# Windowed attention and a spatial-gating MLP on one core: another order of the same instructions, with score and PV groups of head pairs side by side

## The chip, the core and the metric

The kernel runs on one core of a Trainium2 chip. A core has five engines that work at the same time, each with its own queue that it takes strictly in order: TensorE (PE, matrix products; its weight loads are listed apart as PEld), VectorE (DVE), ScalarE (ACT), GpSimd (POOL) and SyncE (SP), which here only issues DMA transfers. Engines wait for each other by semaphores. Operands lie in SBUF; TensorE writes its results to PSUM, from where VectorE and ScalarE read them. The metric is the time of one execution in microseconds (us), as the median of several runs.

## The reference: what is computed

```python
scores = scale * np.matmul(q, k.transpose(0, 1, 3, 2))      # q, k, v: (8, 8, 576, 64), scale = 1/8
mask = (rel >= 0) & (rel < window)                          # rel = query - key, window = 64
scores = np.where(mask, scores, -1000000000.0)
...
attn = attn / (np.sum(attn, axis=-1, keepdims=True) + 1e-09)
return np.matmul(attn, v).astype(np.float32)                # x: (8, 576, 512) after heads are joined

h = np.maximum(x @ w_in, 0.0)                               # w_in: (512, 1024); u, v: its halves
v_n = (v - mu) / np.sqrt(var + 1e-06)                       # over the 512 columns of a row
v_s = np.einsum('ts,bsd->btd', w_spatial, v_n) + b_spatial[None, :, None]
gated = u * v_s
return (gated @ w_out).astype(np.float32)
```

For each of 8 batches: attention with a causal window of 64 positions in 8 heads, and on its result a layer with two weight products, a normalisation and a product over the 576 positions. Inputs and output are float32; the kernel computes its products from float16.

## The kernel before

The program is a list of small pieces of work. A string, ORDER, names 1195 of them as words; a loop at the end of the kernel (L653) takes the words in turn and calls the helper of each, which issues a few instructions. Dependencies are found by the framework from the tiles that are read and written. So ORDER settles one thing only: in which order each engine meets its instructions, each queue its transfers, and each buffer of a ring its tiles. A word ends in a letter where the engine of a copy can be chosen: A for ScalarE, D for VectorE, P for GpSimd.

The words, by stage, with b the batch:

- Loads on SP's queue: `l.b.q.s` and `l.b.k.s` (L297), `lv.b.n` (L313), the halves of w_in `wl.half.r` (L248); on GpSimd's queue `wsp` (w_spatial) and `wout`. `st.b.j` (L636) stores a result tile on SP's queue.
- Casts to float16: `c` (L326; batches 4 to 7 in two pieces of 128x1152, the earlier ones in five of 128x512), `cv` (L339), `wc` (L253). `sh` (L348) makes a copy of V that is shifted by 64 rows.
- Turning q and k so that the head dimension lies on partitions: in batches 0 to 3 by TensorE (`T`, L372, and the copy out of PSUM, `to`), in 4 to 7 by VectorE (`R`, L365).
- Attention, for a pair of heads s = 0 to 3, and s = 4 for the last 64 positions of all heads: `S` (L394) computes scores, with TensorE in 64*64 tiles in batches 0 to 3 and in 32*64 tiles in 4 to 7; `E` (L449, exp, ScalarE), `M` (L463, mask by a minimum, VectorE), `P` (L476) computes the sums of the softmax and the product with V, in tiles of 128*64; `n1`, `n2` (L499, L505, ScalarE) give the inverse of the sum as exp(-ln), `x` (L512, VectorE) multiplies it in.
- The layer: `V` (L526, products of x with the second half of w_in; `Q`, L534, does it for the last 64 positions beside the last `O` of the batch before, in two halves of the array, 128*64), `vo` (relu out of PSUM), `bs` (statistics, VectorE), `rs` (ScalarE), `ln` (normalise, VectorE), `U` (L584, first half of w_in) and `ru` (relu, ScalarE), `G` (L604, product over positions) and `g` (L615, VectorE), `O` (L622, w_out), `oc` (copy out of PSUM).
- `W` and `wo` turn w_spatial once. `H.n` (L641) issues n matmuls on zeros near the start.

`V`, `U`, `G`, `O`, `W` and `T` use TensorE's full 128*128 tile (the last 64 positions of `T` and the last slice of `G` have fewer rows).

Two rings of PSUM set limits to the order. Scores and PV results of s = 0 to 3 (and scores of s = 4) share two buffers with the tag "att", so each `S` or `P` waits until the tile two allocations before it has been read; nearly all else shares four buffers with the tag "mm" (L180).

## Time and profile before

| | |
|---|---|
| median of 11 runs | 212.97 us (211.97 to 213.71) |
| profiled execution, its own time | 214.61 us |
| its span, first to last instruction | 212.9 us |
| busy in it: PE, DVE, ACT, POOL | 199.1, 174.2, 163.7, 65.6 us |
| mean granted TensorE clock | 0.992 |
| start of the first `G` (G.0.1) | 40.96 us |
| DMA traffic | 41.47 MB, mean 195 GB/s |

How to read the lines that follow: `L486` is a line of the kernel; `oz<-e,onesK 128*64 128x512 f16 x2` is two instructions that write tile oz from tiles e and onesK, with 128 rows and 64 columns of the array active (128*64) and an operand of 128 partitions by 512 elements. In a timeline, the first number is the start and the second the time from the first start to the last end in us. TensorE's matmuls overlap: a 128x512 one lasts 0.38 us and the next one starts 0.216 us after it, so that the distance of starts, not the duration, is what one costs. Words and rows are matched by counting: TensorE's 2726 matmuls stand in the trace in ORDER's sequence.

### The profile page before, as it was taken

What the parts mean: (1) busy time and instruction counts of PE and PEld (TensorE: products, weight loads), DVE (VectorE), ACT (ScalarE), POOL (GpSimd) and SP (SyncE); (2) the same over time, 40 slices, a digit from 0 to 9 for tenths busy, and PEclk for the clock granted to TensorE, in tenths of its full rate; (3) what the DMA queues carried; (4) which work ended last, traced back from release to release, by engine and by line L of the source; (5) the groups of instructions that cost most, each with busy time, mean ns of one, the idle gap of its engine ahead of it and who ended that gap; (6) DMA issues with size and microseconds to landing.
All of it is one profiled execution on the core that took longest, in us unless ns stands there. A gap on an engine that the chain in (4) does not pass through costs nothing.

```text
span 212.9 us, 6682 instructions
## 1 busy us (share of the span) xinstructions
PE 199.1 (93%) x2726; PEld 106.9 (50%) x2726; DVE 174.2 (82%) x359; ACT 163.7 (77%) x305; POOL 65.6 (31%) x93
## 2 busy tenths in 40 slices
...
DMA packets 77742, 41.47 MB, mean 195 GB/s; under 512 B 44368, under 2 KB 72080, under 8 KB 77712
## 3 DMA queue, kind: packets, MB, share of 16 engines
...
q0 software_dynamic: 1168, 1.19, 3.7%
...
## 4 chain that ended last, share of the span: by engine, by line
PE 75%; SPq 7%; DVE 6%; ACT 5%; DMA 3%; issue 1%; POOL 1%; DVEq 0%
PE ps L612 19%; PE po L626 13%; PE pv L531 11%; PE pu L589 11%; PE oz L486 4%; SPq L317 4%; PE sc L421 4%; PE oz L496 4%; DMA wf<-in_moe_w_in_dram 3%; PE pv L543 3%; SPq L301 2%; PE sc L410 2%; PE pu L594 2%; DVE st L562 1%; ACT vs L556 1%
## 5 line engine op out<-in xcount | busy, mean ns | idle before, releaser
L612 PE MATMUL ps<-wspT,vn 128*128 128x512 f16 (+1 forms) x256 | 39.0, 286 | 0.6 <-DVE wspT L276 0.6
L453 ACT ACTIVATE e<-sc 128x1024 f16<-128x1024 f32 x32 | 32.6, 1024 | 3.5 <-PE sc L410 3.3
L531 PE MATMUL pv<-win,x 128*128 128x512 f16 x128 | 32.7, 392 | 0.4 <-DVE x L517 0.4
L517 DVE TENSOR_TENSOR x<-oz,zi 128x512 f16<-128x512 f32 (+1 forms) x40 | 25.0, 629 | 8.5 <-ACT zi L509 8.3
L626 PE MATMUL po<-wout,g 128*128 128x512 f16 x128 | 30.8, 379 | 0.0
L589 PE MATMUL pu<-x,win 128*128 128x512 f16 x128 | 30.5, 380 | 0.1
L502 ACT ACTIVATE ln<-oz 128x512 f32<-128x512 f32 (+1 forms) x40 | 21.8, 555 | 9.9 <-PE oz L496 9.9
L562 DVE BATCH_NORM_STATS2 st<-vs 128x6 f32<-128x512 f16 (+1 forms) x40 | 26.9, 674 | 0.5 <-ACT vs L556 0.2
L619 DVE TENSOR_TENSOR g<-ps,ru 128x512 f16<-128x512 f32 (+1 forms) x40 | 24.2, 628 | 3.5 <-PE ps L612 2.2
L469 DVE TENSOR_TENSOR e<-e,mask 128x1024 f16<-128x1024 f16 x32 | 23.3, 728 | 2.9 <-ACT e L453 2.6
L612 PEld LDWEIGHTS <-vn 128*128 128x128 f16 x256 | 17.0, 97 | 14.9 <-DVE vn L580 1.9
L556 ACT ACTIVATE vs<-pv 128x512 f16<-128x512 f32 (+1 forms) x32 | 18.6, 597 | 6.9 <-PE pv L531 6.2
L509 ACT ACTIVATE zi<-ln 128x512 f32<-128x512 f32 (+1 forms) x40 | 23.3, 590 | 0.6
L602 ACT ACTIVATE ru<-pu 128x512 f32<-128x512 f32 (+1 forms) x40 | 21.1, 558 | 2.5 <-PE pu L594 2.0
L360 POOL COPY vs<-vn 64x512 f16<-64x512 f16 (+1 forms) x15 | 13.0, 870 | 22.0 <-DVE vn L346 10.0
L531 PEld LDWEIGHTS <-x 128*128 128x128 f16 x128 | 11.7, 100 | 14.5 <-DVE x L517 1.8
L633 ACT COPY ob<-po 128x512 f32<-128x512 f32 (+1 forms) x21 | 12.1, 587 | 8.7 <-PE po L626 6.5
L589 PEld LDWEIGHTS <-win 128*128 128x128 f16 x128 | 11.7, 98 | 13.1 <-ACT vs L556 0.4
L626 PEld LDWEIGHTS <-g 128*128 128x128 f16 x128 | 11.5, 98 | 12.3 <-DVE g L619 0.7
L612 PE MATMUL ps<-wspT,vlast 65*128 65x512 f16 (+1 forms) x64 | 17.1, 288 | 0.0
L496 PEld LDWEIGHTS <-vn 128*64 128x64 f16 x320 | 13.6, 112 | 3.5
L486 PE MATMUL oz<-e,onesK 128*64 128x512 f16 x64 | 12.8, 396 | 2.4 <-ACT vs L351 1.3
...
## 6 DMA issues: line engine op xcount, KB each, us to landing
...
```

Of the source, the lines that this page charges most:

```text
L453: nc.scalar.activation(e2[:, :, :], sc[0][:, :, :], AF.Exp, bias=0.0, scale=0.125)
L469: nc.vector.tensor_tensor(e2[:, :, :], e2[:, :, :], m, ALU.min)
L496: nc.tensor.matmul(oz[64 * h:64 * h + 64, 0, c0:c0 + 64], vt, e2[:, h, c0:c0 + 64], start=True, stop=True)
L502: nc.scalar.activation(lnz[:, 0:n], OZ[b, s][:, 1, 0:n], AF.Ln)
L509: nc.scalar.activation(zinv[:, 0:n], lnz[:, 0:n], AF.Exp, bias=0.0, scale=-1.0)
L517: nc.vector.tensor_tensor(x[:, 0:n], oz[:, 0, 0:n], zinv[:, 0:n], ALU.mult)
L531: nc.tensor.matmul(PV[b, j][0:jn, :], xcol(b, r, j), w_in_sb[:, r, 512:1024], start=(r == 0), stop=(r == 3))
L562: nc.vector.bn_stats(st6[0:jn, 0:6], VSB[b, j][0:jn, :])
L589: nc.tensor.matmul(pu[:, :], w_in_sb[:, r, 128 * m:128 * m + 128], X[b, r][:, :], start=(r == 0), stop=(r == 3))
L612: nc.tensor.matmul(o, VN[b, kk][0:kn, 128 * mm_:128 * mm_ + 128], w, start=(kk == 0), stop=(kk == 4))
L619: nc.vector.tensor_tensor(g[:, :], ps[:, 0:n], RU.pop((b, m))[:, 0:n], ALU.mult)
L626: nc.tensor.matmul(po[:, :], G[b, r][:, 128 * j:128 * j + 128], w_out_sb[:, r, :], start=(r == 0), stop=(r == 3))
```

## The change

ORDER is replaced by another sequence of the same 1195 pieces of work; no helper changes. From batch 1 on, most score groups `S` of neighbouring head pairs follow each other directly in TensorE's order, and so do the PV groups `P` (`S.5.0 S.5.1`, `P.5.1 P.5.0`). Everything else moves with it: the other work of TensorE, the loads and stores in SP's queue, and the order on each engine. For 151 of the 285 copies and casts the engine is another one; by word, VectorE does 14 `to` in place of 25, 16 `vo` in place of 8, 5 `wc` in place of 1; ScalarE 26 `to` in place of 15 and 24 `vo` in place of 32.

The diff, cut to the start, two places in batches 5 to 7, and the end:

```diff
ORDER = """
-id scratch table l.0.q.1 keep H.2 l.0.q.0 mask l.0.k.3 H.3 l.0.k.0 small l.0.k.1 lv.0.0 H.3 lv.0.1
-c.0.q.1.A l.0.q.2 H.4 lv.0.3 c.0.q.0.P lv.0.4 H.2 l.0.k.2 T.0.q.0 T.0.q.1 to.0.q.0.A H.2 wl.1.1
-c.0.k.1.D c.0.k.0.A lv.0.2 to.0.q.1.A T.0.k.0 l.0.q.3 T.0.k.1 maskr to.0.k.0.D H.3 wl.1.0 to.0.k.1.D
-S.0.0 l.0.q.4 c.0.q.2.P cv.0.0.D E.0.0 S.0.1 lv.0.5 c.0.k.3.D E.0.1 sh.0.0.0.D T.0.k.3 l.0.k.4
-T.0.q.2 H.6 to.0.q.2.D sh.0.0.1.A c.0.k.2.P M.0.0 lv.1.0 P.0.0 cv.0.1.D M.0.1 n1.0.0 lv.0.7 T.0.k.2
-sh.0.1.0.A to.0.k.3.D lv.0.6 to.0.k.2.A sh.0.1.1.D P.0.1 c.0.q.3.D n2.0.0 lv.0.8 H.4 n1.0.1 x.0.0
-wl.1.3 n2.0.1 T.0.q.3 wl.1.2 cv.0.2.D S.0.2 c.0.q.4.A l.1.k.1 x.0.1 c.0.k.4.P to.0.q.3.A wl.0.3
-T.0.q.4 sh.0.2.1.D wc.1.1.P E.0.2 l.1.q.0 T.0.k.4 S.0.3 to.0.k.4.D to.0.q.4.D wl.0.2 wc.1.0.A M.0.2
-S.0.4 cv.0.3.P E.0.3 wl.0.0 V.0.3.0.1 V.0.3.1.2 l.1.k.0 sh.0.3.1.D sh.0.2.0.A P.0.2 cv.0.4.D E.0.4
-M.0.3 n1.0.2 V.0.0.0.1 M.0.4 V.0.0.1.2 wc.1.2.P V.0.2.0.1 sh.0.4.0.A V.0.2.1.2 sh.0.3.0.P P.0.3
-n2.0.2 n1.0.3 wc.1.3.P x.0.2 P.0.4 n2.0.3 wsp c.1.k.1.D wl.0.1 V.0.2.2.3 V.0.0.2.3 n1.0.4 lv.1.1
-x.0.3 V.0.3.2.3 n2.0.4 l.1.q.1 c.1.q.0.A wc.0.3.D V.0.3.3.4 lv.1.3 x.0.4 V.0.2.3.4 vo.0.3.A
-V.0.0.3.4 vo.0.2.D l.1.q.2 wc.0.0.A V.0.1.0.1 l.1.k.2 bs.0.3 V.0.1.1.2 vo.0.0.A V.0.1.2.3 l.1.k.3
-V.0.1.3.4 wc.0.2.A wc.0.1.P T.1.q.0 lv.1.2 vo.0.1.A Q.0 to.1.q.0.D c.1.k.0.P U.0.0 l.1.q.3 vo.0.4.A
-cv.1.0.D U.0.4 bs.0.2 ru.0.0 T.1.k.0 U.0.3 sh.1.0.1.D to.1.k.0.A bs.0.4 c.1.q.1.P ones.0 S.1.0
-ru.0.4 sh.1.0.0.D U.0.2 E.1.0 bs.0.0 l.1.k.4 U.0.1 bs.0.1 ru.0.3 ru.0.2 T.1.q.1 M.1.0 T.1.k.1 ru.0.1
-W.1 to.1.q.1.D rs.0 lv.1.5 W.0 wo.1.A ln.0.4 P.1.0 ln.0.2 to.1.k.1.A c.1.q.2.P W.4 wo.0.D n1.1.0
-lv.1.4 ln.0.1 S.1.1 W.2 ln.0.3 n2.1.0 ln.0.0 l.1.q.4 T.1.q.2 wo.4.A W.3 wo.2.D c.1.k.3.P E.1.1
-wo.3.D G.0.1 lv.1.6 wout x.1.0 lv.1.7 ones.1 to.1.q.2.D c.1.k.2.P G.0.4 l.2.k.0 M.1.1 T.1.k.2 G.0.2
...
-ru.4.3 l.6.q.4 G.4.0 x.5.1 E.5.2 l.6.k.2 cv.6.1.D S.5.4 M.5.2 S.5.3 st.3.4 E.5.4 g.4.0 G.4.2 E.5.3
-l.6.k.7 l.6.k.4 G.4.3 cv.6.2.A M.5.3 l.6.k.6 M.5.4 P.5.3 cv.6.3.D l.6.q.5 g.4.2 P.5.4 n1.5.3
-sh.6.1.1.P P.5.2 n1.5.4 g.4.3 O.4.1 n2.5.3 lv.6.0 sh.6.1.0.P n2.5.4 x.5.3 l.7.k.0 O.4.2 n1.5.2
-c.6.q.0.D oc.4.1.A c.6.k.0.P O.4.3 n2.5.2 x.5.4 st.4.1 oc.4.2.D l.7.k.2 U.5.4 x.5.2 l.7.k.1 G.4.4
-ru.5.4 c.6.k.1.P l.7.k.3 oc.4.3.A R.6.q.0 O.4.0 st.3.3 g.4.4 V.5.1.0.4 l.7.q.0 R.6.k.0 sh.6.4.0.P
-oc.4.0.D V.5.2.0.4 st.4.2 vo.5.1.A c.6.q.1.A bs.5.1 l.7.q.7 S.6.0 S.6.1 lv.7.2 R.6.k.1 E.6.0
...
-sh.7.1.1.P l.7.q.5 g.5.3 O.5.0 l.7.q.4 g.5.4 sh.7.4.0.P R.7.q.0 S.6.4 O.5.1 cv.7.1.P E.6.4 x.6.3
-sh.7.1.0.A oc.5.0.D S.7.1 M.6.4 S.7.0 oc.5.1.A c.7.k.1.D P.6.4 cv.7.0.P V.6.2.0.4 n1.6.4 E.7.0
-sh.7.0.1.P O.5.2 n2.6.4 vo.6.2.A x.6.4 V.6.1.0.4 oc.5.2.A M.7.0 U.6.4 R.7.k.1 st.5.2 vo.6.1.A
-V.6.3.0.4 st.4.0 E.7.1 bs.6.1 st.5.1 V.6.0.0.4 st.5.0 c.7.q.1.A sh.7.0.0.D P.7.0 Q.6 R.7.q.1 n1.7.0
-vo.6.0.A M.7.1 ru.6.4 S.7.2 vo.6.3.A oc.5.4.D U.6.2 E.7.2 bs.6.0 U.6.0 vo.6.4.A bs.6.2 ru.6.2 U.6.3
-bs.6.3 n2.7.0 ru.6.0 O.5.3 bs.6.4 ru.6.3 U.6.1 x.7.0 rs.6 ln.6.0 P.7.1 ln.6.2 ln.6.1 n1.7.1 S.7.3
-ln.6.3 oc.5.3.A ln.6.4 G.6.2 M.7.2 E.7.3 st.5.3 G.6.1 n2.7.1 g.6.2 ru.6.1 M.7.3 G.6.0 g.6.1 x.7.1
-G.6.3 g.6.0 S.7.4 g.6.3 O.6.0 E.7.4 M.7.4 P.7.2 oc.6.0.D P.7.3 P.7.4 G.6.4 n1.7.4 n1.7.2 O.6.1
-n2.7.4 n2.7.2 x.7.4 O.6.2 n1.7.3 oc.6.1.D g.6.4 n2.7.3 U.7.4 st.6.1 x.7.2 Q.7 st.5.4 ru.7.4 x.7.3
-oc.6.2.D V.7.0.0.4 vo.7.4.D st.6.2 V.7.1.0.4 bs.7.4 oc.6.4.A V.7.3.0.4 vo.7.0.A vo.7.1.D bs.7.0
-V.7.2.0.4 bs.7.1 O.6.3 vo.7.2.A vo.7.3.A bs.7.2 U.7.0 oc.6.3.A bs.7.3 U.7.2 st.6.3 st.6.0 rs.7 U.7.3
-st.6.4 ru.7.0 ln.7.3 U.7.1 ln.7.1 ru.7.3 ln.7.0 ln.7.2 ru.7.2 ln.7.4 G.7.2 ru.7.1 G.7.0 g.7.2 G.7.1
-g.7.0 G.7.3 g.7.1 G.7.4 g.7.3 O.7.0 g.7.4 O.7.1 oc.7.0.A st.7.0 O.7.2 oc.7.1.A st.7.1 O.7.3 oc.7.2.D
-st.7.2 Q.8 oc.7.3.D st.7.3 oc.7.4.A st.7.4
+keep l.0.k.0 mask l.0.q.0 maskr l.0.q.1 l.0.k.1 scratch table H.3 l.0.k.3 lv.0.1 l.0.q.2 H.4 lv.0.0
+c.0.k.0.P l.0.k.2 c.0.q.0.P l.0.q.3 H.2 id c.0.q.1.P lv.0.2 T.0.q.0 T.0.k.0 lv.0.3 to.0.q.0.A H.2
+c.0.k.1.A l.0.q.4 ones.1 T.0.k.1 to.0.k.0.A to.0.k.1.D c.0.k.3.A S.0.0 lv.0.4 small c.0.q.2.A
+T.0.q.1 H.3 to.0.q.1.D E.0.0 l.0.k.4 H.3 cv.0.0.D wl.1.1 c.0.k.2.D sh.0.0.1.P H.2 sh.0.0.0.D T.0.k.2
+c.0.q.3.A lv.0.5 S.0.1 M.0.0 wl.1.0 T.0.k.3 E.0.1 wl.1.2 P.0.0 cv.0.1.P lv.0.8 n1.0.0 M.0.1
+sh.0.1.1.P lv.0.7 c.0.q.4.A sh.0.1.0.D P.0.1 n2.0.0 lv.0.6 to.0.k.3.D to.0.k.2.A T.0.q.3 ones.0
+wl.0.2 T.0.q.2 c.0.k.4.D H.6 x.0.0 n1.0.1 wl.1.3 to.0.q.2.A to.0.q.3.D n2.0.1 wc.1.1.D T.0.q.4 S.0.2
+wc.1.0.P wl.0.0 x.0.1 T.0.k.4 E.0.2 H.4 wl.0.1 wc.1.2.D cv.0.2.D l.1.q.0 to.0.k.4.A S.0.3 to.0.q.4.D
+cv.0.4.D wl.0.3 V.0.2.0.1 E.0.3 V.0.2.1.2 M.0.2 S.0.4 l.1.k.0 V.0.0.0.1 sh.0.2.0.D V.0.0.1.2
+sh.0.4.0.A sh.0.2.1.D l.1.q.1 P.0.2 M.0.3 E.0.4 l.1.q.2 cv.0.3.D n1.0.2 sh.0.3.1.D n2.0.2 l.1.k.1
+sh.0.3.0.D P.0.3 M.0.4 n1.0.3 lv.1.1 wc.0.0.P x.0.2 P.0.4 n2.0.3 wsp wc.1.3.D lv.1.0 V.0.0.2.3
+V.0.3.0.1 x.0.3 V.0.3.1.2 V.0.3.2.3 c.1.q.0.A V.0.2.2.3 wc.0.1.D lv.1.2 V.0.0.3.4 wc.0.2.D n1.0.4
+V.0.2.3.4 V.0.3.3.4 vo.0.0.D vo.0.2.A n2.0.4 vo.0.3.D V.0.1.0.1 wc.0.3.A V.0.1.1.2 V.0.1.2.3 x.0.4
+c.1.k.0.A T.1.q.0 bs.0.3 V.0.1.3.4 to.1.q.0.A Q.0 U.0.0 c.1.q.1.D vo.0.1.A l.1.k.4 vo.0.4.A bs.0.1
+U.0.3 ru.0.0 bs.0.0 U.0.4 ru.0.3 T.1.k.0 bs.0.2 ru.0.4 T.1.q.1 c.1.k.1.P U.0.1 c.1.q.2.A to.1.k.0.A
+bs.0.4 T.1.k.1 ru.0.1 lv.1.3 U.0.2 to.1.q.1.D rs.0 lv.1.5 to.1.k.1.A ln.0.1 S.1.0 l.1.k.2 ln.0.4
+ru.0.2 S.1.1 ln.0.0 l.1.q.3 E.1.0 W.1 ln.0.3 ln.0.2 lv.1.4 W.0 wo.1.A T.1.q.2 cv.1.0.D l.1.q.4 W.3
+M.1.0 sh.1.0.0.A sh.1.0.1.P W.2 l.1.k.3 wo.0.D wo.3.A P.1.0 to.1.q.2.D c.1.k.4.P lv.1.7 wo.2.A W.4
+wout E.1.1 wo.4.D G.0.1 cv.1.1.P n1.1.0 lv.1.6 G.0.4 g.0.1 sh.1.1.0.P l.2.q.0 n2.1.0 G.0.2 lv.1.8
...
+E.5.2 g.4.0 G.4.2 lv.6.0 E.5.3 M.5.2 S.5.4 G.4.3 E.5.4 M.5.3 l.6.k.7 c.6.k.0.A M.5.4 P.5.3 g.4.2
+lv.7.3 P.5.2 cv.6.4.D P.5.4 n1.5.2 g.4.3 sh.6.4.0.P lv.7.2 O.4.2 n1.5.4 c.6.q.0.D cv.6.2.P n2.5.2
+G.4.4 n2.5.4 x.5.2 st.3.3 n1.5.3 O.4.3 cv.6.0.P st.3.4 x.5.4 n2.5.3 R.6.q.0 l.6.k.4 O.4.0 oc.4.2.A
+l.6.q.5 g.4.4 x.5.3 U.5.4 l.6.q.6 oc.4.0.A V.5.0.0.4 l.6.k.5 oc.4.3.D sh.6.1.0.A l.6.q.4 cv.6.1.D
+V.5.1.0.4 l.7.q.5 vo.5.0.D sh.6.0.0.P ru.5.4 R.6.k.0 V.5.2.0.4 st.4.2 vo.5.1.A sh.6.1.1.P l.6.k.6
+bs.5.0 S.6.0 vo.5.2.A lv.7.0 S.6.1 bs.5.1 cv.7.2.A cv.7.3.P Q.5 l.7.q.2 E.6.1 sh.6.0.1.P bs.5.2
+l.7.k.0 V.5.3.0.4 oc.4.4.A M.6.1 sh.7.1.1.P E.6.0 vo.5.4.D O.4.1 l.7.q.1 bs.5.4 vo.5.3.A U.5.2
+sh.7.1.0.P oc.4.1.A bs.5.3 U.5.1 lv.7.1 ru.5.2 M.6.0 rs.5 l.7.k.1 P.6.1 ru.5.1 ln.5.4 st.4.0 P.6.0
+ln.5.1 n1.6.1 st.4.3 ln.5.2 U.5.3 n2.6.1 ln.5.0 l.7.q.3 ln.5.3 c.6.k.1.A c.6.q.1.D G.5.0 l.7.q.0
+x.6.1 st.4.1 n1.6.0 U.5.0 R.6.q.1 ru.5.3 l.7.q.6 G.5.1 R.6.k.1 ru.5.0 n2.6.0 g.5.0 l.7.q.4 cv.7.1.P
+G.5.2 cv.7.0.A x.6.0 l.7.q.7 g.5.1 S.6.2 l.7.k.5 g.5.2 S.6.4 E.6.2 G.5.3 l.7.k.2 E.6.4 l.7.k.3 S.6.3
+g.5.3 lv.7.4 G.5.4 E.6.3 M.6.4 M.6.2 O.5.0 M.6.3 P.6.2 oc.5.0.D P.6.3 n1.6.2 c.7.q.0.D P.6.4 n1.6.3
+O.5.2 g.5.4 n2.6.2 n2.6.3 O.5.1 x.6.2 n1.6.4 x.6.3 n2.6.4 V.6.3.0.4 oc.5.2.A x.6.4 c.7.k.0.P
+oc.5.1.A U.6.3 vo.6.3.D c.7.q.1.A st.5.1 bs.6.3 V.6.2.0.4 st.4.4 ru.6.3 l.7.k.4 R.7.q.1 V.6.0.0.4
+sh.7.0.1.A l.7.k.6 R.7.q.0 l.7.k.7 V.6.1.0.4 vo.6.2.A st.5.0 R.7.k.0 O.5.3 st.5.2 vo.6.1.A bs.6.2
+vo.6.0.A S.7.1 cv.7.4.D S.7.0 sh.7.0.0.D E.7.1 sh.7.4.0.D Q.6 bs.6.1 oc.5.3.A M.7.1 U.6.4 oc.5.4.A
+st.5.3 c.7.k.1.P bs.6.0 U.6.2 vo.6.4.A E.7.0 bs.6.4 U.6.0 M.7.0 rs.6 U.6.1 ru.6.4 ln.6.0 ru.6.2
+ln.6.2 P.7.1 ln.6.1 P.7.0 n1.7.1 ln.6.4 ln.6.3 n1.7.0 G.6.0 R.7.k.1 n2.7.1 n2.7.0 G.6.1 x.7.1 ru.6.0
+x.7.0 ru.6.1 S.7.3 g.6.1 S.7.2 E.7.3 G.6.2 g.6.0 E.7.2 M.7.3 G.6.3 M.7.2 S.7.4 g.6.2 P.7.2 E.7.4
+g.6.3 O.6.2 n1.7.2 M.7.4 n2.7.2 P.7.3 x.7.2 P.7.4 n1.7.3 O.6.1 oc.6.2.D n2.7.3 G.6.4 n1.7.4 st.6.2
+x.7.3 n2.7.4 V.7.0.0.4 x.7.4 g.6.4 V.7.2.0.4 oc.6.1.D vo.7.0.D V.7.3.0.4 vo.7.2.D V.7.1.0.4 bs.7.2
+O.6.3 vo.7.1.A vo.7.3.A Q.7 oc.6.3.A bs.7.3 st.6.3 U.7.2 bs.7.0 oc.6.4.A st.5.4 vo.7.4.A U.7.4
+bs.7.1 U.7.1 ru.7.4 bs.7.4 ru.7.2 U.7.3 rs.7 ru.7.1 U.7.0 ln.7.4 ln.7.3 ln.7.2 O.6.0 ru.7.0 ln.7.0
+ln.7.1 ru.7.3 G.7.0 oc.6.0.A st.6.0 G.7.1 g.7.0 st.6.1 st.6.4 G.7.2 G.7.3 g.7.2 g.7.1 G.7.4 g.7.3
+O.7.0 O.7.1 oc.7.0.D g.7.4 O.7.2 st.7.0 oc.7.1.D O.7.3 st.7.1 oc.7.2.A st.7.2 Q.8 oc.7.3.D st.7.3
+oc.7.4.A st.7.4
 """
```

TensorE's own words from `T.1.q.0` on, before:

```
T.1.q.0 Q.0 U.0.0 U.0.4 T.1.k.0 U.0.3 S.1.0 U.0.2 U.0.1 T.1.q.1 T.1.k.1 W.1 W.0 P.1.0 W.4 S.1.1 W.2 T.1.q.2 W.3 G.0.1 G.0.4 T.1.k.2 G.0.2 T.1.k.3
G.0.0 S.1.2 P.1.1 T.1.q.4 T.1.k.4 G.0.3 T.1.q.3 P.1.2 O.0.2 O.0.0 S.1.3 S.1.4 O.0.3 O.0.1 T.2.q.0 T.2.k.0 P.1.3 V.1.1.0.2 V.1.3.0.2 V.1.3.2.3 P.1.4
S.2.0 V.1.1.2.3 V.1.1.3.4 V.1.3.3.4 U.1.1 V.1.2.0.2 V.1.0.0.2 T.2.k.1 V.1.0.2.3 V.1.2.2.3 V.1.2.3.4 T.2.q.1 V.1.0.3.4 P.2.0 Q.1 S.2.1 T.2.k.2 T.2.q.2
U.1.4 U.1.2 U.1.3 U.1.0 T.2.q.4 S.2.2 P.2.1 T.2.q.3 T.2.k.3 G.1.0 G.1.1 G.1.3 S.2.3 T.2.k.4 P.2.2 G.1.2 G.1.4 P.2.3 S.2.4 O.1.1 O.1.2 V.2.2.0.4
T.3.q.0 O.1.0 P.2.4 T.3.k.0 V.2.1.0.4 V.2.0.0.4 O.1.3 V.2.3.0.4 T.3.k.2 T.3.k.1 T.3.q.1 S.3.0 Q.2 S.3.1 T.3.q.2 U.2.2 T.3.k.3 P.3.0 S.3.2 T.3.q.3
U.2.0 U.2.1 U.2.3 T.3.q.4 T.3.k.4 P.3.2 P.3.1 U.2.4 G.2.3 G.2.1 G.2.0 S.3.4 S.3.3 G.2.2 G.2.4 O.2.1 O.2.0 P.3.3 O.2.2 O.2.3 V.3.0.0.4 V.3.3.0.4 P.3.4
S.4.0 S.4.1 V.3.2.0.4 V.3.1.0.4 U.3.0 Q.3 P.4.0 S.4.2 U.3.1 U.3.2 U.3.3 U.3.4 P.4.1 S.4.3 G.3.1 G.3.0 P.4.2 P.4.3 G.3.2 G.3.3 G.3.4 O.3.1 O.3.2 O.3.0
S.4.4 V.4.1.0.4 V.4.2.0.4 S.5.0 S.5.1 P.4.4 U.4.0 V.4.0.0.4 V.4.3.0.4 P.5.0 Q.4 P.5.1 U.4.4 U.4.2 U.4.1 O.3.3 U.4.3 G.4.1 S.5.2 G.4.0 S.5.4 S.5.3
G.4.2 G.4.3 P.5.3 P.5.4 P.5.2 O.4.1 O.4.2 O.4.3 U.5.4 G.4.4 O.4.0 V.5.1.0.4 V.5.2.0.4 S.6.0 S.6.1 V.5.3.0.4 V.5.0.0.4 S.6.2 Q.5 P.6.0 U.5.1 U.5.0
U.5.3 P.6.1 S.6.3 U.5.2 G.5.0 G.5.2 P.6.2 P.6.3 G.5.1 G.5.3 G.5.4 O.5.0 S.6.4 O.5.1 S.7.1 S.7.0 P.6.4 V.6.2.0.4 O.5.2 V.6.1.0.4 U.6.4 V.6.3.0.4
V.6.0.0.4 P.7.0 Q.6 S.7.2 U.6.2 U.6.0 U.6.3 O.5.3 U.6.1 P.7.1 S.7.3 G.6.2 G.6.1 G.6.0 G.6.3 S.7.4 O.6.0 P.7.2 P.7.3 P.7.4 G.6.4 O.6.1 O.6.2 U.7.4 Q.7
V.7.0.0.4 V.7.1.0.4 V.7.3.0.4 V.7.2.0.4 O.6.3 U.7.0 U.7.2 U.7.3 U.7.1 G.7.2 G.7.0 G.7.1 G.7.3 G.7.4 O.7.0 O.7.1 O.7.2 O.7.3 Q.8
```

and after:

```
T.1.q.0 V.0.1.3.4 Q.0 U.0.0 U.0.3 U.0.4 T.1.k.0 T.1.q.1 U.0.1 T.1.k.1 U.0.2 S.1.0 S.1.1 W.1 W.0 T.1.q.2 W.3 W.2 P.1.0 W.4 G.0.1 G.0.4 G.0.2 T.1.k.2
G.0.0 S.1.2 P.1.1 T.1.q.3 G.0.3 T.1.k.3 P.1.2 T.1.q.4 T.1.k.4 O.0.2 S.1.3 O.0.0 O.0.3 S.1.4 P.1.3 O.0.1 V.1.2.0.2 P.1.4 V.1.2.2.3 V.1.0.0.2 V.1.2.3.4
V.1.0.2.3 V.1.0.3.4 V.1.1.0.2 V.1.1.2.3 V.1.1.3.4 T.2.q.1 T.2.q.0 V.1.3.0.2 V.1.3.2.3 V.1.3.3.4 T.2.k.1 T.2.k.0 Q.1 S.2.0 S.2.1 U.1.4 U.1.3 T.2.k.2
U.1.2 U.1.1 P.2.0 P.2.1 U.1.0 T.2.q.2 T.2.k.3 G.1.0 T.2.q.3 G.1.1 T.2.k.4 T.2.q.4 S.2.2 G.1.2 S.2.3 S.2.4 G.1.4 G.1.3 P.2.2 P.2.3 O.1.1 O.1.3 O.1.0
O.1.2 T.3.k.0 P.2.4 V.2.0.0.4 V.2.1.0.4 T.3.q.1 V.2.2.0.4 V.2.3.0.4 T.3.k.1 T.3.q.0 Q.2 S.3.1 S.3.0 U.2.4 T.3.q.2 U.2.0 U.2.2 U.2.1 U.2.3 T.3.k.2
T.3.q.3 P.3.0 P.3.1 T.3.k.3 G.2.0 G.2.1 T.3.q.4 T.3.k.4 S.3.2 G.2.2 S.3.3 S.3.4 G.2.4 G.2.3 P.3.2 P.3.3 O.2.0 O.2.3 P.3.4 O.2.1 V.3.0.0.4 V.3.2.0.4
Q.3 S.4.0 S.4.1 V.3.3.0.4 V.3.1.0.4 U.3.0 U.3.4 U.3.2 P.4.1 P.4.0 U.3.3 U.3.1 O.2.2 G.3.2 G.3.0 G.3.1 S.4.2 S.4.3 G.3.3 S.4.4 O.3.0 P.4.2 P.4.3 G.3.4
O.3.2 P.4.4 O.3.1 V.4.1.0.4 V.4.3.0.4 V.4.2.0.4 V.4.0.0.4 Q.4 S.5.0 S.5.1 U.4.3 O.3.3 U.4.2 U.4.0 U.4.1 P.5.1 P.5.0 U.4.4 G.4.1 G.4.0 S.5.2 S.5.3
G.4.2 S.5.4 G.4.3 P.5.3 P.5.2 P.5.4 O.4.2 G.4.4 O.4.3 O.4.0 U.5.4 V.5.0.0.4 V.5.1.0.4 V.5.2.0.4 S.6.0 S.6.1 Q.5 V.5.3.0.4 O.4.1 U.5.2 U.5.1 P.6.1
P.6.0 U.5.3 G.5.0 U.5.0 G.5.1 G.5.2 S.6.2 S.6.4 G.5.3 S.6.3 G.5.4 O.5.0 P.6.2 P.6.3 P.6.4 O.5.2 O.5.1 V.6.3.0.4 U.6.3 V.6.2.0.4 V.6.0.0.4 V.6.1.0.4
O.5.3 S.7.1 S.7.0 Q.6 U.6.4 U.6.2 U.6.0 U.6.1 P.7.1 P.7.0 G.6.0 G.6.1 S.7.3 S.7.2 G.6.2 G.6.3 S.7.4 P.7.2 O.6.2 P.7.3 P.7.4 O.6.1 G.6.4 V.7.0.0.4
V.7.2.0.4 V.7.3.0.4 V.7.1.0.4 O.6.3 Q.7 U.7.2 U.7.4 U.7.1 U.7.3 U.7.0 O.6.0 G.7.0 G.7.1 G.7.2 G.7.3 G.7.4 O.7.0 O.7.1 O.7.2 O.7.3 Q.8
```

## The prediction

> **What bounds the kernel now.** I read the page first, for shares and the chain that ended last.
>
> ```profile
> PE 199.1 (93%) x2726; PEld 106.9 (50%) x2726; DVE 174.2 (82%) x359; ACT 163.7 (77%) x305; POOL 65.6 (31%) x93
> PE 75%; SPq 7%; DVE 6%; ACT 5%; DMA 3%; issue 1%; POOL 1%; DVEq 0%
> ```
>
> TensorE (PE) is busy 93% and holds 75% of the chain. Next, busy time by stretch (start:end, length, then busy and count for PE, PEld, DVE, ACT, POOL, granted clock, DMA share, GB/s):
>
> ```profile
> 24.00:28.00 4.00, 2.64 (x32) 1.19 (x33) 2.28 (x6) 2.68 (x7) 4.00 (x6) 0.73 0.98 291
> 28.00:32.00 4.00, 4.00 (x18) 1.65 (x19) 3.50 (x8) 3.49 (x7) 2.09 (x4) 0.84 1.09 211
> 45.00:55.00 10.00, 10.00 (x151) 5.53 (x148) 9.68 (x19) 8.07 (x14) 1.56 (x4) 1.00 0.82 209
> ```
>
> Up to 28 us PE starves; from 45 us it is full at full clock. "Full" hides the cost that the change aims at, so the third view is PE's timeline (start, duration, operation, count), read by the distance from one start to the next:
>
> ```profile
> 89.98 0.41 PE L486 MATMUL oz<-e,onesK 128*64 128x512 f16 x2
> ...
> 90.47 0.39 PE L486 MATMUL oz<-e,onesK 128*64 128x512 f16 x2
> ...
> 91.04 0.64 PE L594 MATMUL pu<-x,win 128*128 128x64 f16 x16
> ...
> 97.03 1.89 PE L626 MATMUL po<-wout,g 128*128 128x512 f16 x8
> 98.85 0.41 PE L486 MATMUL oz<-e,onesK 128*64 128x512 f16 x2
> ...
> 99.44 1.90 PE L626 MATMUL po<-wout,g 128*128 128x512 f16 x8
> 101.18 1.89 PE L531 MATMUL pv<-win,x 128*128 128x512 f16 x8
> 103.35 0.99 PE L421 MATMUL sc<-tr 32*64 32x128 f16 x64
> 104.27 1.90 PE L531 MATMUL pv<-win,x 128*128 128x512 f16 x8
> ...
> 108.42 0.66 PE L421 MATMUL sc<-tr 32*64 32x128 f16 x32
> 109.02 2.76 PE L589 MATMUL pu<-x,win 128*128 128x512 f16 x12
> ```
>
> Eight 128x512 matmuls take 1.82 us before a PV group (97.03 to 98.85) and 1.74 before a full-width one (99.44 to 101.18, with 0.01 of re-entry): entering the 128*64 shape costs 0.09 ahead of the group. A lone PV group takes 0.59 (98.85 to 99.44), two in a row 0.49 + 0.57. With 0.10 at the borders, two lone groups cost 1.38, a pair 1.16: a pair saves 0.22 us. Batches 4 to 7's score groups (32*64): lone 0.60 + 0.10, pair 0.92 + 0.10: a pair saves 0.38.
>
> The fourth view is the chain before 28 us:
>
> ```profile
> 17.75 6.19 DMA wf<-in_moe_w_in_dram
> 24.00 0.85 POOL win L254
> 24.85 0.56 POOL vs L358
> 25.46 0.40 PE oz L496 x12
> 27.17 0.70 DVE x L517
> ```
>
> A weight cast waiting for its DMA stands in GpSimd's queue ahead of the shifted V copy that P.0.3 needs.
>
> **The change, part by part.** The profiled execution took 214.61 us, 212.9 of it span, 1.7 around it; the median of the runs is 212.97, so this execution is 1.6 us slow. I sum differences within it and put the result on the median.
>
> (a) Shape changes on PE. From T.1.q.0 on I counted in both orders each place where the next group has another shape. Between full width and 128*64 or 64*64 one change costs 0.11 (0.225 for in and out; the 64*64 scores give the same: 0.35 alone at 45.4 us, 0.25 where another follows at 10.0): 57 before, 63 after. Between PV and 64*64 scores 0.12 (0.10 at the end of one, 0.02 at the start of the other): 8 and 4. Into the 32-row scores 0.20: 15 and 12; out of them 0.17: 15 and 12. Sums: 6.27+0.96+3.00+2.55 = 12.8 and 6.93+0.48+2.40+2.04 = 11.85. The change is worth -0.9 us, not 0.2 to 0.4 for each of its pairs: the order before often has a PV group of one pair beside a score group of the next, which saves one border too, and the new order gives those up. Pricing full-width matmuls at 0.216 us apart and groups from such rows, PE's list from G.0.1 to the end comes to 165.8 us before and 164.9 after. As PE is full, this lies on the path. Its end can only be smaller if waits fill it; I keep 0 and -0.9 as ends, and take -0.9.
>
> (b) Start, up to G.0.1 (40.96 us). The same groups precede G.0.1 in both orders, so its start measures the stage. In SP's queue wl.1.2 moves from 24th to 19th load, lv.0.6 from 21st to 22nd, l.1.q.0 stays 27th; its cast c.1.q.0.A now stands on ScalarE ahead of n1.0.4 and so of x.0.4, Q.0. On the loads' spacing here (lv.0.6 issued at 15.3, cast at 22.05) it lands near 22.9. wc.1.2 goes to VectorE, which it holds until about 20; GpSimd's 0.85 + 0.61 us ahead of P.0.3 are gone, but cv.0.3, both sh.0.3 and M.0.4 now run on VectorE. Adding 0.42, 0.29, 0.29 and the score/normaliser rows (0.60, 0.63, 0.69), x.0.3 ends near 27.2 against 27.86 here. What is late next: l.1.q.0, issued near 21.8 and landing near 26.5, holds n1.0.4; then the w_spatial load (issued 26.15, 9.8 us to land; now behind wc.0.0 on GpSimd, so at about the same time) holds W.1 (36.72 here), the VectorE chain ln, cv.1.0, M.1.0, and P.1.0, which W.4 now follows. The first groups move too: scratch is cleared behind the six mask operations, so warm-up matmuls start near 3.2 instead of 1.26, and T.0.k.2 and S.0.1 come 2 us later. I cost this at nothing, because P.0.1 waits for V data until 15.66 anyway; without that cover it would be up to +2. Row by row I get G.0.1 at 39.9 to 41. Ends: -1.7 (all of the GpSimd wait) and +1.0 (l.1.q.0 lands an issue slot or two later). Nearest is the row-by-row walk, -0.8; since this execution is slow where the clock row says 0.73, I take -0.5.
>
> (c) Waits on PE from G.0.1 to 190 us. Against the price list PE loses 2.1 us here: 0.91 before U.5.4 (near 144), 0.32 after U.5.3 (155.5), 0.22 after U.1.4, 0.17 before G.4.1, the rest under 0.12 each. The change replaces all of them. Pairing makes cycles longer: the four PSUM slots of two shared by scores and PV ("att") must both turn over. After a pair, the second x needs 0.25+0.60+0.60+0.63+0.63+0.68 = 3.4 us from the first group's end, 2.8 from the second's. The new order's PE work leaves 2.7 to 3.2 at S.7.2, S.5.3 and V.6.3: up to 0.2 each. S to P needs 2.2 (0.4+1.02+0.7); S.1.0 leaves 1.8, S.1.3 and S.6.3 2.1. From the last V or Q to the first G (relu, statistics, ln) it leaves 5.9 to 6.9 us in batches 1 to 4 against 4.5 to 7.4 before, but 4.6 and 4.2 in 5 and 6, where adding the queues gives 0.45 and 0.1 of wait. Loads: score groups now come 10 to 20 us behind the issue of their last input against 7 to 13, so no new wait on SP's queue. Sum of the tight places 1.5 to 3.5; I take 2.3, so +0.2. Ends -1.5 and +2.0.
>
> (d) End. After V.7.1, O.6.3 and Q.7 the work U.7.2 to O.6.0 covers 4.8 us. bs.7.1 and bs.7.4 come last on VectorE (0.83 apart), then rs (0.55) and five ln (0.35), ln.7.0 fourth: G.7.0 waits 0.3, V.7.3 0.1 for oc.6.1. Before, G.7.2 found its operands ready. I take +0.4, ends 0 and +0.8. The stores st.6.1 and st.6.4 now queue behind st.6.0, but land (3.0 us) before oc.7.1 and oc.7.3 need their buffers.
>
> Elsewhere engines swap copies (11 PSUM copies of `to` go from VectorE to ScalarE, 8 `vo` the other way): no cost while both have 18% to spare.
>
> Sum: -0.9 -0.5 +0.2 +0.4 = -0.8, so 212.2 us.
>
> **A row that speaks against it.** Three long casts stood on VectorE; four do now, c.6.q.0, c.6.q.1 and c.7.q.0 ahead of x.
>
> ```profile
> 143.04 1.14 POOL L337 CAST nk<-fk 128x1152 f16<-128x1152 f32 x1
> 143.17 1.63 DVE L337 CAST nq<-fq 128x1152 f16<-128x1152 f32 x1
> 144.72 0.41 DVE L517 TENSOR_TENSOR x<-oz,zi 128x256 f16<-128x256 f32 x1
> ```
>
> Beside a GpSimd cast it took 1.63 us; the two alone took 0.75. This is the 0.91 wait of (c). The Trainium skill, "SBUF — State Buffer", section "Who interferes with whom", goes further: a VectorE copy or cast in a two-port mode and any GpSimd instruction exclude each other for the whole instruction. By that rule every one of the roughly nine fp16 copies and casts that VectorE gains is exposed, not these casts alone; at GpSimd's 31% busy and half of a 0.9 us hold each, that estimate adds 1.3 us of VectorE time, and the sum would be 213.5 if all of it reached PE, 212.2 by the row. I go by the row: most of these copies are early ones, with slack behind them.
>
> **Rivals.**
> A, slower: the long casts in line. c.6.q.1 stands directly before x.6.1, R.6.q.1, R.6.k.1 and x.6.0, which S.6.2 and S.6.4 need, and c.7.q.0 before x.6.2 and x.6.3, which V.6.3 needs. At 1.63 each the waits grow by 0.9 + 0.9: 212.2 + 1.8 = 214.0. For it: the 0.91 wait exists. Against: GpSimd's list has fewer casts there. It decides once the two together run 1.3 us long.
> B, slower: the start. ScalarE stands at c.1.q.0 until 28 us, so +1.0 in place of -0.5: 213.7. For it: ACT's queue has n1.0.4, vo.0.2 and wc.0.3 behind that cast.
> C, no change: the 0.9 us of shape changes return as waits on the two slots: 213.0.
> D, faster still: no wait like that of 144 us (-0.9 more), start -0.9: 210.9.
>
> **How the numbers follow.** Forecast 212.2: 0.40; D 0.10; C 0.15; A 0.20; B 0.15. A measurement tells about 0.2% (0.43 us) from no change. Faster 0.50 (forecast and D), same 0.15 (C), slower 0.35 (A, B). The range runs from 210.7, just past D, to 214.3, just past A; the sum of all bad ends (216.8) and of all good ones (208.9) lies outside. The forecast's own range is 211.4 to 212.8.
>
> **What would show it.** (a) PE's starts from G.0.1 to the end, without waits, 0.9 us less; pairs 1.06 and 0.92 long. (b) G.0.1 near 40.5, its weight and x rows earlier. (c) PE waits of about 2.3 us, the largest at S.6.4 and G.5.0. (d) G.7.0 waiting on vn by 0.3. The prediction is wrong if waits after 41 us exceed 3.5 us, if casts of 1152 columns on VectorE run near 1.6 us, or if G.0.1 starts after 42.

## The result and the profile after

The changed kernel took 217.52 us (median of 12 runs, 215.53 to 219.62), the kernel before 212.79 in the runs beside it (47). The ratio is 1.0187, with a 95% interval of 1.0162 to 1.0213: 1.9% slower, outside the predicted range of 210.7 to 214.3, and away from the forecast gain. Medians here are over all runs, ratios leave out those over 1.5% above the fastest of the same kernel, without which the changed kernel's median is 216.90. So versions are compared by their ratios below, and a difference in us is that of the ratios on a kernel of 213 us: the change costs 4.0 us.

The mean granted clock differs between executions of the changed kernel: three of the twelve with 0.998 or more took 216.1 to 216.6 us, six with 0.988 to 0.991 took 215.5 to 219.0, three with 0.984 or less 218.9 to 219.6. The profiled execution is one of the last (218.94 us, clock 0.984).

The page after, busy time and the shares of the chain:

```profile
PE 200.7 (92%) x2726; PEld 106.2 (49%) x2726; DVE 172.2 (79%) x361; ACT 167.3 (77%) x308; POOL 64.5 (30%) x89
PE 60%; SPq 12%; DMA 11%; ACT 8%; DVE 5%; issue 2%; POOL 1%; ACTq 0%; POOLq 0%
```

PE is as busy as before, but holds 60% of the chain in place of 75%. What grew are SP's queue (7 to 12%) and transfers (3 to 11%). The stretches of the start and the same steady stretch as before (columns as in the prediction):

```profile
24.00:28.00 4.00, 3.08 (x22) 1.25 (x22) 3.50 (x8) 2.93 (x7) 2.43 (x4) 1.00 0.61 127
28.00:32.00 4.00, 2.54 (x14) 1.02 (x13) 0.97 (x3) 0.60 (x1) 0.00 (x0) 1.00 1.15 270
32.00:36.00 4.00, 1.91 (x9) 0.81 (x9) 1.82 (x4) 2.56 (x6) 0.62 (x1) 0.58 1.17 255
36.00:40.00 4.00, 4.00 (x35) 2.66 (x33) 2.32 (x7) 2.56 (x6) 0.00 (x0) 0.57 0.94 230
45.00:55.00 10.00, 8.57 (x131) 4.99 (x130) 7.54 (x15) 7.33 (x14) 3.80 (x5) 1.00 1.10 257
```

From 24 to 28 us the DMA engines have spare time (0.61, against 0.98 before). From 28 to 36 us ScalarE, VectorE and PE all stand still for long, and from 32 to 40 the clock is near half. The chain of the changed kernel names what began it, and a second place later:

```profile
18.64 4.77 DMA wf<-in_moe_w_in_dram
23.41 0.05 issue
23.46 0.90 POOL win L254
24.36 0.02 issue
24.38 0.33 SPq L251
24.70 0.04 issue
24.75 1.65 SPq L301
...
44.20 9.25 DMA wout<-in_moe_w_out_dram
53.45 0.05 issue
53.49 1.04 PE po L626 x4
```

Its timeline, in order of time (SP's, ScalarE's and PE's rows; in brackets the idle time before a row and what ended it):

```profile
20.64 0.43 SPq L301 DMA_DIRECT2D fq<-in_q_dram  x1
24.38 0.33 SPq L251 DMA_DIRECT2D wf<-in_moe_w_in_dram  x1
24.75 1.65 SPq L301 DMA_DIRECT2D fk<-in_k_dram  x1
...
29.50 1.04 PE L589 MATMUL pu<-x,win 128*128 128x512 f16 x4
...
32.93 0.62 ACT L331 CAST nk<-fk 128x512 f16<-128x512 f32 x1 [4.33 <-DMA fk<-in_k_dram]
33.46 0.58 ACT L388 COPY tr<-tp_0q 128x512 f16<-128x512 f16 x1
...
34.09 1.86 PE L589 MATMUL pu<-x,win 128*128 128x512 f16 x4 [3.55 <-ACT tr L388]
```

This is one story. The eight halves of w_in go through a ring of five buffers. The load wl.0.3 (24.38) waits until wl.0.0 has landed (23.41) and GpSimd has cast it (24.36), so SP's queue issues nothing from 21.07 to 24.38. Behind it stands l.1.k.0, issued at 24.75 where it had been at 22.79 before; it took 1.65 us to issue and landed at 32.91. That is 8.2 us from the start of its issue, against 5.4 before, so the load was not only late but slow. The w_spatial load of 576 KB leaves GpSimd's queue just ahead of it, at 24.30, which may be the reason. It stays open: in two profiles with this start and the same distance l.1.k.0 took 7.4 us, in another (c.1.k.0 on GpSimd, below) 5.1. Its cast c.1.k.0 is the next step of ScalarE, which idles 4.33 us in front of it. Behind the cast stands the copy to.1.q.0, which empties one of the four PSUM buffers "mm" that U.0.3 needs. So PE, with all operands there, waits 3.55 us, and is then given half the clock. G.0.1 starts at 44.33 us, 3.37 later than in the profile of before.

These are single executions, and a start moves between them. Five profiles whose words up to G.0.1 are those of before have it at 39.05 to 40.96 us (middle 39.93), four with the changed start, or that start with three words added or four matmuls repeated, at 41.65 to 44.33. The two groups don't overlap, so the later start is not chance.

SP's rows of before, for comparison (the loads l.1.k.0 and wl.0.1):

```profile
22.79 0.38 SPq L301 DMA_DIRECT2D fk<-in_k_dram  x1
24.88 0.33 SPq L251 DMA_DIRECT2D wf<-in_moe_w_in_dram  x1
```

The profiled executions compare as follows. "List" is PE's price list from G.0.1 to the end, as in the prediction; waits are what PE's starts lose against it; the rest (before G.0.1 and after the last matmul's start) is 5.7 in both. Where a wait is given by a group's name alone, it lies between that group's start and the start of the next.

| | own time | G.0.1 | list | waits |
|---|---|---|---|---|
| before | 214.61 | 40.96 | 165.83 | 2.15 |
| changed | 218.94 | 44.33 | 164.93 | 4.02 |
| difference | +4.33 | +3.37 | -0.90 | +1.87 |

### The profile page after: what moved, and what is told of

Its sections match the earlier page's. It is cut to its first block, busy times and chain, and to the rows that moved or that the text cites. A ratio compares the mean times of both kernels' runs of the same rounds, so it can differ in the third digit from the quotient of the medians.

```text
span 217.2 us, 6700 instructions
## 1 busy us (share of the span) xinstructions
PE 200.7 (92%) x2726; PEld 106.2 (49%) x2726; DVE 172.2 (79%) x361; ACT 167.3 (77%) x308; POOL 64.5 (30%) x89
## 4 chain that ended last, share of the span: by engine, by line
PE 60%; SPq 12%; DMA 11%; ACT 8%; DVE 5%; issue 2%; POOL 1%; ACTq 0%; POOLq 0%
PE ps L612 14%; PE po L626 13%; PE pv L531 9%; PE pu L589 8%; SPq L301 5%; SPq L317 5%; DMA wf<-in_moe_w_in_dram 4%; DMA wout<-in_moe_w_out_dram 4%; PE sc L421 4%; PE oz L486 3%; PE oz L496 3%; PE pv L543 2%; DMA vf<-in_v_dram 2%; SPq L305 2%; DVE st L562 1%
## 5 line engine op out<-in xcount | busy, mean ns | idle before, releaser
L612 PE MATMUL ps<-wspT,vn 128*128 128x512 f16 (+1 forms) x256 | 38.5, 286 | 0.0
L589 PE MATMUL pu<-x,win 128*128 128x512 f16 x128 | 32.8, 395 | 3.9 <-ACT tr L388 3.5
L626 PE MATMUL po<-wout,g 128*128 128x512 f16 x128 | 31.7, 380 | 1.4 <-DMA wout<-in_moe_w_out_dram 1.4
L531 PE MATMUL pv<-win,x 128*128 128x512 f16 x128 | 30.9, 380 | 0.9 <-ACT vs L556 0.5
L469 DVE TENSOR_TENSOR e<-e,mask 128x1024 f16<-128x1024 f16 x32 | 22.6, 713 | 2.6 <-ACT e L453 2.4
L612 PEld LDWEIGHTS <-vn 128*128 128x128 f16 x256 | 16.3, 97 | 13.0 <-DVE vn L580 1.6
L360 POOL COPY vs<-vn 64x512 f16<-64x512 f16 (+1 forms) x16 | 14.2, 893 | 24.6 <-DVE vn L343 20.7
L633 ACT COPY ob<-po 128x512 f32<-128x512 f32 (+1 forms) x23 | 13.3, 581 | 9.6 <-PE po L626 8.4
L556 ACT ACTIVATE vs<-pv 128x512 f16<-128x512 f32 (+1 forms) x24 | 13.9, 597 | 8.5 <-PE pv L531 6.3
L337 POOL CAST nk<-fk 128x1152 f16<-128x1152 f32 x6 | 7.3, 1213 | 31.3 <-DMA fk<-in_k_dram 24.2
```

What stands on the lines that cost most here:

```text
L469: nc.vector.tensor_tensor(e2[:, :, :], e2[:, :, :], m, ALU.min)
L531: nc.tensor.matmul(PV[b, j][0:jn, :], xcol(b, r, j), w_in_sb[:, r, 512:1024], start=(r == 0), stop=(r == 3))
L589: nc.tensor.matmul(pu[:, :], w_in_sb[:, r, 128 * m:128 * m + 128], X[b, r][:, :], start=(r == 0), stop=(r == 3))
L612: nc.tensor.matmul(o, VN[b, kk][0:kn, 128 * mm_:128 * mm_ + 128], w, start=(kk == 0), stop=(kk == 4))
L626: nc.tensor.matmul(po[:, :], G[b, r][:, 128 * j:128 * j + 128], w_out_sb[:, r, :], start=(r == 0), stop=(r == 3))
```

## Experiments

Theory START: the time is lost before G.0.1, by the stop of SP's queue and what stands behind it. Theory PAIRS: the waits of the new steady order cost more than its shape changes bring. Later two more were formed on the steady part, and they are named where they come up. Ratios are to the kernel before, run on the same chip. The diffs show only the words around an edit, with the lines broken anew.

**The two halves exchanged.** First the order of before up to G.0.1 followed by the changed order, then the reverse; eight words that cross the cut are put in at the seam.

```diff
 (order of before) ... wo.3.D G.0.1
-(order of before from here on)
+(changed order from here on)
```

> The words of the order before up to G.0.1, and from there the changed order (eight words that stand on the other side of that cut keep the changed order's sequence). Theory START (the changed order loses only ahead of G.0.1, by ScalarE standing at the cast of l.1.k.0, and gains 0.7 us behind it): G.0.1 near 41 us and a time 0.5 to 1.3 us under before, about 212.0. Theory PAIRS (the paired part itself loses through the two shared PSUM buffers): 1 us or more above before, 213.8 or more.

Measured: 213.69 us (ratio 1.0038, 1.0004 to 1.0071), 0.8 above before: between the two forecasts. G.0.1 starts at 37.93 in its profile.

> The opposite splice: the changed order up to G.0.1, the order before from there. START: G.0.1 near 44.3 us and 4 to 5.5 us above before, 217 to 218. PAIRS: within 1.5 us of before.

Measured: 218.12 us (1.0238, 1.0185 to 1.029), as START had it. The changed start costs 5.1 us ahead of the steady part of before and 3.2 ahead of the changed one; the changed steady part costs 0.8 with the start of before. So the start carries the loss, and the steady part brings nothing: its list is 0.9 shorter, but in the profile of the first hybrid PE waits 4.39 us after G.0.1. Not all of the 5.1 lies ahead of G.0.1: in the second hybrid's profile (an execution of 223.22 us) PE stands 2.5 us in front of T.1.k.2, behind G.0.1, for a cast of GpSimd.

**The pairs taken apart**, 23 of those behind G.0.1, everything else left.

```diff
-c.2.k.2.P S.2.0 S.2.1 lv.2.5 oc.0.4.A sh.2.1.1.P bs.1.3 U.1.4 E.2.1
+c.2.k.2.P S.2.0 lv.2.5 oc.0.4.A sh.2.1.1.P bs.1.3 U.1.4 S.2.1 E.2.1
```

> The changed order with 23 of its pairs behind G.0.1 taken apart: the second S or P changes places with the full-width group after it in TensorE's order; all other work keeps its place. The price list of shape changes gives TensorE 5.2 us more to issue. If these prices hold and TensorE stays full, the time is 4 to 5.5 us above the changed kernel (221 to 223). If shape changes hide in waits or cost less in place, under 2 us above it.

Measured: 225.56 us (1.0565, 1.0499 to 1.0631), 8.0 above the changed kernel and more than expected. 5.2 of it is the price list; the rest goes with longer waits (10.9 in its profile, an execution of 228.28 us). That they come from an order that was made around pairs is argued, not shown. The pairs as such are not what made the change slow: without them it is slower still.

**One load moved.** wl.0.3 goes behind l.1.k.1 in SP's queue.

```diff
-to.0.q.4.D cv.0.4.D wl.0.3 V.0.2.0.1
+to.0.q.4.D cv.0.4.D V.0.2.0.1
-n2.0.2 l.1.k.1 sh.0.3.0.D
+n2.0.2 l.1.k.1 wl.0.3 sh.0.3.0.D
```

> The changed order with one transfer moved: wl.0.3, which waits in SP's queue for the cast wc.0.0 to free a buffer, goes behind l.1.k.0, l.1.q.1, l.1.q.2 and l.1.k.1. START with SP's queue as its first cause: these loads are issued from 21 us on instead of 24.8, c.1.k.0 on ScalarE starts 3 us earlier, unless the cast wc.0.3 ahead of it now waits for wl.0.3; TensorE's wait at U.0.3 falls from 3.6 us to under 1.5 and the time by 2 to 4 us, to 213.5 to 215.5. If the DMA engines and not the queue's order set the landing, the time stays at 217.5.

Measured: 213.96 us (1.0027, 0.9992 to 1.0062): 3.4 of the 4.0 us are back. Its timeline:

```profile
20.09 0.47 SPq L301 DMA_DIRECT2D fk<-in_k_dram  x1
23.46 0.34 SPq L251 DMA_DIRECT2D wf<-in_moe_w_in_dram  x1
...
29.67 0.61 ACT L331 CAST nk<-fk 128x512 f16<-128x512 f32 x1
30.19 0.58 ACT L388 COPY tr<-tp_0q 128x512 f16<-128x512 f16 x1
...
30.82 1.02 PE L589 MATMUL pu<-x,win 128*128 128x512 f16 x4 [0.24 <-ACT tr L388]
```

l.1.k.0 leaves at 20.09, the cast no longer waits for it, U.0.3 waits 0.24 in place of 3.55, the clock stays full, and G.0.1 starts at 39.05. A stop of SP's queue is still there (from 22.10 to 23.46), with nothing urgent behind it.

**The cast moved instead of the load**: c.1.k.0 on GpSimd, the load as late as before.

```diff
-x.0.4 c.1.k.0.A T.1.q.0
+x.0.4 c.1.k.0.P T.1.q.0
```

> The changed order with one cast moved: c.1.k.0 from ScalarE to GpSimd, so that the copy to.1.q.0 no longer stands behind it. The load l.1.k.0 stays late (near 32.9 us). Theory QUEUE (the time was lost because other work stood behind the waiting cast): U.0.3 starts near 31, T.1.k.0 behind U.0.4 waits for the cast instead, and 1 to 3 us come back: 214.5 to 216.5. Theory LOAD (the late load alone decides, whoever waits for it): W.1 stays near 41 us and the time at 217 to 218.

Measured: 215.71 us (1.0112, 1.0064 to 1.016), 1.6 back, as QUEUE had it. The copy and U.0.3 now run at once, and PE stops a few groups later for the next late load, l.1.q.1, which VectorE casts:

```profile
30.32 0.62 POOL L331 CAST nk<-fk 128x512 f16<-128x512 f32 x1 [3.50 <-DMA fk<-in_k_dram]
...
34.99 0.40 PE L378 MATMUL tp_1q<-id,nq 128*128 128x128 f16 x4 [2.50 <-DVE nq L331]
```

How the loss divides between the copy that stood behind the cast and the late loads is not settled by this: l.1.k.0 wasn't near 32.9 here, as was expected, but had landed by 30.32, so a cast on ScalarE would have been free earlier as well.

**PE kept busy in the gap.** U.0.0's four matmuls are given out five times; each time the sum begins anew.

```diff
+            for _ in range(5 if (b, m) == (0, 0) else 1):
                 for r in range(4):
                     nc.tensor.matmul(pu[:, :], ...)
```

> The changed order, with the four matmuls of U.0.0 given out five times (the sums are begun anew each time, so only the last counts): TensorE is busy for about 3.5 us of the gap of 3.7 us behind U.0.0. If the half clock from 32.6 to 39.4 us comes from that gap, the matmuls of U.0.3 to U.0.2 run at full rate again and the time falls by 1.5 to 3 us: 214.5 to 216. If the half clock comes from something else, or costs nothing because the groups wait for data anyway: 217.3 to 218.

Measured: 217.23 us (1.0199, 1.0153 to 1.0245), 0.3 above the changed kernel by the ratios, so the expected gain isn't there. In its profiled execution no half clock falls into the start (the start, by stretch):

```profile
32.00:36.00 4.00, 4.00 (x37) 2.13 (x35) 2.01 (x6) 2.98 (x6) 0.60 (x1) 1.00 1.06 254
36.00:40.00 4.00, 3.35 (x56) 1.93 (x53) 3.66 (x11) 3.57 (x10) 0.02 (x1) 1.00 1.01 232
```

That one took 216.59 us, with G.0.1 at 42.71. The executions of the changed kernel with a full clock take the same without the extra matmuls (216.1 to 216.6), and two of the three other runs of this version have a mean clock of 0.992. The profile of the version without pairs has the same start without the extra matmuls, a wait of 2.08 us at U.0.3, and no half clock before G.0.1 (41.65). So that the extra matmuls kept the clock up isn't shown. What the half clock costs can be read from the profiles: U.0.3 to G.0.1 takes 10.24 us in the changed kernel, with two windows of 3.41 us at half rate, 9.32 in the second hybrid with one, and 8.23 here and in the version with wl.0.3 moved with none. That is about 1 us a window, 2.0 in the profile of the changed kernel. The wait alone, at full clock, already costs more than 3 (216.1 to 216.6 against 212.79).

**wout earlier as well.** The chain's second place is T.1.k.4 to O.0.2, 1.32 us in the kernel with wl.0.3 moved, which ends with the load of w_out. It now goes out right behind w_spatial.

```diff
-n2.0.3 wsp wc.1.3.D
+n2.0.3 wsp wout wc.1.3.D
-W.4 wout E.1.1
+W.4 E.1.1
```

> The changed order with two loads moved in SP's queue: wl.0.3 behind l.1.k.1 (alone: 213.96 us, with 1.32 us of wait left at T.1.k.4, ended by the wout load), and wout directly behind the w_spatial load. If that wait is the wout load's: it goes, and the time is 1.0 to 1.4 less, 212.5 to 213.0. Rival (DMA): wout takes DMA time from the loads of batch 1 and what is gained at T.1.k.4 is lost before G.0.1, which then starts after 39.5 us: 213.5 to 214.5.

Measured: 213.39 us (1.0025, 0.9989 to 1.006). The wait is gone and G.0.1 stays at 39.14, so the rival falls too, yet the ratio is the one without this step (1.0027). In the profiles the waits fell from 4.4 to 3.2, with others longer (V.6.3 0.57 in place of 0.48, U.1.1 0.32 in place of under 0.15); over the runs no gain is left of that. The change with its start mended is as fast as the kernel before, and not faster.

**The steady part, first attempt: late pairs only.** The order of before up to G.4.1, the changed order from there.

```diff
 (order of before) ... G.4.1
-(order of before from here on)
+(changed order from here on)
```

> The order of before up to G.4.1, the changed order from there, so that only batches 5 to 7 are paired in the new way. By the price list its groups from G.0.1 on come to 165.3 us against 165.8 before and 164.9 in the changed order. Theory PAIRS-EARLY (the waits of the new order lie in batches 1 to 3; its batches 5 to 7 wait 0.7 us where the order of before waits 1.5): 165.3 + 1.3 against 165.8 + 2.1, so 1.3 us less than before: 211.2 to 212.0. Rival (queues in general: any new neighbourhood of casts and exps costs about what the shape changes bring): 212.7 to 213.5.

Measured: 214.58 us (1.0059, 1.0028 to 1.009), worse than either expectation. In its profile the list is 0.5 shorter than before and the waits 3.13; 1.4 of them lie at the seam (G.4.1, G.4.0, O.4.3). That the waits lie in batches 1 to 3 is not borne out.

**Second attempt: three steps out of the way.** In two kernels, the changed order with both loads moved and the first hybrid, three steps of VectorE that stand ahead of a waiting pair or group are moved back or forward.

```diff
-G.1.3 cv.2.4.D E.2.4 lv.3.5 M.2.3
+G.1.3 E.2.4 lv.3.5 M.2.3 cv.2.4.D
-S.3.0 bs.2.3 U.2.4 E.3.1 T.3.q.2 U.2.0 vo.2.4.D
+S.3.0 vo.2.4.D bs.2.3 U.2.4 E.3.1 T.3.q.2 U.2.0
-n1.6.2 c.7.q.0.D P.6.4 n1.6.3 O.5.2 ... x.6.2 n1.6.4 x.6.3
+n1.6.2 P.6.4 n1.6.3 O.5.2 ... x.6.2 n1.6.4 x.6.3 c.7.q.0.D
```

> The changed order with the two loads moved (alone: 213.39 us) and three steps of VectorE taken out of a queue in front of a pair: cv.2.4 behind M.2.3 (P.2.2 waited 0.47 us), vo.2.4 ahead of bs.2.3 (U.2.0 waited 0.45), c.7.q.0 behind x.6.3 (V.6.3 waited 0.57). Theory QUEUES (the waits that ate the gain in shape changes are single steps in front of the pairs on VectorE): those three waits fall under 0.15 each and the time to 211.9 to 212.6, below the kernel before. Rival SLOTS (a pair needs its two PSUM slots turned over, whatever stands in the queues): the waits move to the next group and the time stays at 213.0 to 213.6.

Measured: 215.99 us (1.0119, 1.0064 to 1.0174), 2.0 worse than without the three moves.

> The order of before up to G.0.1, then the changed order (alone: 213.69 us), with the same three steps moved. QUEUES: 212.3 to 212.9; P.2.2 and V.6.3 lose their waits of 0.47 and 0.22. SLOTS: 213.4 to 214.0.

Measured: 215.28 us (1.0107, 1.0062 to 1.0152), 1.5 worse. Neither forecast holds: V.6.3 still waits 0.48 and 0.21 without the cast in front, P.2.2 0.65 in the first (0.16 in the second), U.2.0's wait is gone, and new waits of 0.4 to 0.6 stand at T.3.k.3, G.2.0 and P.3.2. The timeline of the changed order with the moves shows what is new:

```profile
94.68 0.61 POOL L346 CAST vn<-vf 128x512 f16<-128x512 f32 x1
94.78 2.60 DVE L469 TENSOR_TENSOR e<-e,mask 128x1024 f16<-128x1024 f16 x2
...
95.23 1.60 POOL L337 CAST nq<-fq 128x1152 f16<-128x1152 f32 x1
...
97.43 0.41 PE L486 MATMUL oz<-e,onesK 128*64 128x512 f16 x2 [0.35 <-DVE e L469]
```

Two masks, 0.68 each when GpSimd is idle, take 2.60 us beside two casts of GpSimd, and P.3.3 (97.43) waits for the second of them. So I took all VectorE steps of eleven profiled executions and split them by whether a copy or cast of GpSimd ran at the same time (count, mean us; the longest in brackets):

| VectorE step | GpSimd idle | beside GpSimd |
|---|---|---|
| mask, 128x1024, fp16, both operands in SBUF | 235, 0.68 | 117, 0.83 (1.63) |
| ln, 128x512, fp16 to fp16 in SBUF | 318, 0.40 | 34, 0.66 (0.77) |
| shifted copy of V of L358, 64x512, fp16 in SBUF | 42, 0.27 | 21, 0.63 (0.70) |
| cast 128x1152 in SBUF | 25, 0.75 | 16, 1.14 (2.72) |
| x, 128x512, one operand in PSUM | 213, 0.68 | 139, 0.68 (0.69) |
| copy out of PSUM, 128x512 | 90, 0.68 | 27, 0.67 (0.69) |
| statistics, 128x512, one operand | 170, 0.68 | 182, 0.67 (0.70) |

Theory HOLD: GpSimd's copies hold VectorE's steps of the upper four rows, and PE waits for these.

**GpSimd loaded more**, in the kernel before: 40 copies that nothing depends on.

```diff
+    def k_gz():
+        nc.gpsimd.tensor_copy(junk[:], scratch[:])
...
+gz oc.3.0.A V.4.1.0.4 l.5.q.4 R.5.k.0 E.4.4
```

> The kernel before with 40 copies of a 128x512 fp16 tile added on GpSimd, spread evenly from G.0.1 to Q.7; no step reads what they write. GpSimd is busy for about 24 us more, of 31% busy. Theory HOLD (VectorE's fp16 steps are held while GpSimd copies): about 30% of VectorE's time from G.0.1 on is in such steps, half a copy each, so its steps run 3 to 6 us longer in sum (2.7 to 3.1 us before), the waits on TensorE from G.0.1 on grow from 2.1 to 2.9 us to 4 to 6, and the time to 214.5 to 217. Rival FREE (GpSimd's spare time costs nothing): 212.6 to 213.4.

Measured: 216.03 us (1.0149, 1.0089 to 1.0209): 3.0 us more, from copies on the engine with the most spare time. In its profile PE waits 4.60 us behind G.0.1, and VectorE's steps are held for 7.4 us in sum (3.1 in the profile of before). Some 0.5 of the 2.5 us of added wait is for GpSimd's own casts and copies, which stand behind the added ones (0.30 at T.2.k.2, the rest in front of PV products); the large ones, at O.4.3 and G.4.1, are for VectorE. The largest wait, with its causes (this kernel's line numbers are 6 higher):

```profile
142.79 2.19 DVE L343 CAST nq<-fq 128x1152 f16<-128x1152 f32 x1
143.22 1.14 POOL L343 CAST nk<-fk 128x1152 f16<-128x1152 f32 x1
144.31 1.13 POOL L224 COPY junk<-scratch 128x512 f16<-128x512 f16 x1
...
145.36 0.64 PE L600 MATMUL pu<-x,win 128*128 128x64 f16 x16 [1.30 <-DVE x L523]
```

The added copy runs right behind GpSimd's own cast, and VectorE's cast, which has to wait out more of them, takes 2.19 us (1.63 before).

**Copies taken from GpSimd**, in the changed order with both loads moved: the 26 shifted copies of V behind G.0.1 on VectorE.

```diff
-sh.2.1.1.P bs.1.3 U.1.4
+sh.2.1.1.D bs.1.3 U.1.4
```

> The changed order with the two loads moved (alone: 213.39 us), and the 26 shifted copies of V that GpSimd makes behind G.0.1 (0.61 us each) made by VectorE instead (0.28 each): 16 us less on GpSimd, 7.3 more on VectorE. HOLD: the sum by which VectorE's steps are held falls from 5.1 to 2.5 to 3.5 us, the waits on TensorE from 3.2 to 2 to 2.7, and the time to 212.2 to 213.0. FREE: VectorE's 7.3 us more make the waits longer: 213.6 to 215.

Measured: 220.75 us (1.0347, 1.0301 to 1.0392), 6.9 more than without. The sum of held time was 4.3 us, above the 2.5 to 3.5 expected, and PE's waits grew to 10.0, the longest for masks that come late in VectorE's queue (the list of waits; us in total, times, longest):

```profile
PE oz L486 <- DVE e L469: 4.1, 4, 2.7
```

So this tells nothing for HOLD, and little against it; it shows that VectorE, 82% busy, has no room for 7 us in that order.

**The held cast moved**, in the kernel before.

```diff
-n1.5.2 c.6.q.0.D oc.4.1.A c.6.k.0.P O.4.3 n2.5.2 x.5.4 st.4.1 oc.4.2.D l.7.k.2 U.5.4 x.5.2
+n1.5.2 oc.4.1.A c.6.k.0.P O.4.3 n2.5.2 x.5.4 st.4.1 oc.4.2.D l.7.k.2 U.5.4 x.5.2 c.6.q.0.D
```

> The kernel before with the cast c.6.q.0 moved behind x.5.4 and x.5.2 on VectorE. In the profile of before it ran 1.63 us beside a GpSimd cast (0.75 without) and U.5.4 waited 0.92 us behind it. If that wait is the cast's: it goes, and the time is 0.5 to 0.9 us less, 212.0 to 212.5. Rival: R.6.q.0 and S.6.0 take the wait over, and the time stays within 0.2% of before.

Measured: 212.43 us (ratio 0.9977, 0.9951 to 1.0003). The cast now runs between two GpSimd casts and takes 0.75, and U.5.4 starts without a wait:

```profile
142.58 0.63 PE L594 MATMUL pu<-x,win 128*128 128x64 f16 x16
142.67 0.69 DVE L517 TENSOR_TENSOR x<-oz,zi 128x512 f16<-128x512 f32 x1
143.27 0.75 DVE L337 CAST nq<-fq 128x1152 f16<-128x1152 f32 x1
```

It is the fastest version here, 0.5 us below the kernel before and 4.5 below the changed one, though its interval just includes no gain.

**The kernel before once more.**

> The kernel before, profiled once more. Its first profiled execution took 214.61 us with G.0.1 at 40.96; the median is 212.9. If the 1.7 us between them lie in the start, G.0.1 comes at 39.0 to 39.8 in an execution near the median, and the waits behind it stay at 1.9 to 2.4 us. If they lie in the steady part, G.0.1 stays near 41 and the waits fall under 1 us.

Measured: 214.29 us, G.0.1 at 39.93, waits 2.86. Neither: this execution was nearly as slow as the first, with the time put together differently (start 1.0 earlier, waits 0.7 longer). So the start of one and the same program moves by 1 us between executions (the first had a half-rate window in its start, this one none), and the single profile of before is no exact base for either term.

The profiled executions and HOLD (us; "held" is the sum over VectorE's steps behind 41 us that ran more than 0.06 longer than the idle-GpSimd mean of their kind):

| | waits on PE | held on VectorE |
|---|---|---|
| before, cast moved | 1.8 | 3.3 |
| before, first and second profile | 2.1, 2.9 | 3.1, 2.7 |
| before, 40 copies added | 4.6 | 7.4 |
| changed | 4.0 (1.5 of it for wout) | 3.7 |
| changed, wl.0.3 later | 4.4 (1.3 for wout) | 4.1 |
| changed, both loads moved | 3.2 | 5.1 |
| changed, c.1.k.0 on GpSimd | 3.5 (1.0 for wout) | 3.9 |
| changed, U.0.0 given out five times | 3.3 | 5.8 |
| order of before up to G.4.1, then changed | 3.1 | 3.2 |
| start of before, then changed | 4.4 | 5.3 |
| the same, three steps moved | 5.0 | 5.6 |
| both loads moved, three steps moved | 5.2 | 6.3 |

The changed order's steps are held more, and its waits are mostly longer, but not in step: 3.3 us of wait go with 5.8 held, and 4.4 with 5.3. That holding lengthens the waits is shown by the added copies. The moved cast fits it, but that cast would be out of the way of U.5.4 also if nothing had held it, and the sum of held time did not fall. That holding explains the changed order's extra waits is not shown: the only attempt to take it away there failed for another reason, so this stays open.

## Why the prediction was wrong, point by point

**Step (a), shape changes, -0.9: right in price.** The counts of 57 and 63 changes to and from full width come out as 54 and 60 from G.0.1 on, so the difference, which is all that the sum uses, stands. Pairs cost what the list says. In the changed kernel's timeline two PV groups take 0.49 + 0.57 from start to start, as predicted:

```profile
114.12 0.41 PE L486 MATMUL oz<-e,onesK 128*64 128x512 f16 x2
114.61 0.39 PE L486 MATMUL oz<-e,onesK 128*64 128x512 f16 x2
115.18 1.90 PE L589 MATMUL pu<-x,win 128*128 128x512 f16 x8
```

Whole batches run on the list: from Q.3 to Q.4 the changed kernel took 23.77 us, the list says 23.74. But "I keep 0 and -0.9 as ends, and take -0.9" was the wrong end: waits filled it.

**Step (b), the start, -0.5: this is the step that failed.** Measured in the two profiles +3.4, outside its ends of -1.7 and +1.0; by the hybrids the start costs 3.2 to 5.1 us. It named l.1.q.0 as what is late next, "issued near 21.8 and landing near 26.5", and put the other loads on the spacing that the trace of before showed. That spacing has its own waits for buffers in it, at other loads. In the changed order wl.0.0, wl.0.1 and wl.0.3 wait for one; the queue wasn't walked past them one by one, and l.1.k.0 and l.1.q.1, right behind wl.0.3, weren't priced at all. l.1.q.0 itself left at 20.64, ahead of the stop, and harmed nothing. The row that could have told was shown in the prediction's own fourth view: a load of w_in that takes 6.19 us to land, and its cast on GpSimd, done at 24.85. I booked the end of that wait as a gain for P.0.3 and didn't ask which load sits on the same buffer. It is wl.0.1, which left at 24.88 in the same trace: SP's queue stood for it from 23.17 on. Before, that cost little: l.1.q.1, behind it, was used by TensorE only at 35.98. The price was wrong once more because in the profile the clock was halved behind the stop (2.0 us), which the prediction nowhere counted.

**Step (c), waits from G.0.1 on, +0.2: mis-sized.** Taken 2.3, measured 4.0, just inside the upper end (2.1 and 2.0 more). 1.5 of it is the wout load, which was not in the sum at all: the changed order puts it on GpSimd behind a shifted copy of V that waits 6.84 us for VectorE's cast (cv.1.0), and it left at 44.20, against 38.65 before:

```profile
42.63 0.94 POOL L360 COPY vs<-vn 64x512 f16<-64x512 f16 x1 [6.84 <-DVE vn L343]
...
44.20 0.79 POOL L263 DMA_DIRECT2D wout<-in_moe_w_out_dram  x1
```

Without it 2.5 in that profile and 3.1 to 5.2 in the variants with a good start. The other largest were not at S.6.4 and G.5.0 (0.17 and under 0.1) but at P.2.2 (0.44) and U.2.0 (0.45).

**Step (d), the end, +0.4: wrong, 0.** G.7.0 found its operands ready.

Of the three signs of being wrong, two came: waits of 4.0 us after 41 us, and G.0.1 after 42. The casts of 1152 columns did not run near 1.6.

**The rivals.** B was nearest: the start, ScalarE standing behind a cast that waits for a load. But it was l.1.k.0's cast, not l.1.q.0's, and the price +1.0 for the start in place of +3.4 (profile), so that it pointed at the right engine was partly luck. A, the long casts: c.7.q.0 and its like ran 0.74 to 0.90 in the profile of the changed kernel, so it didn't decide; with another start one of them took 1.42, beside a GpSimd cast. It goes with what GpSimd does at that moment, which shifts from run to run. C, the gain returning as waits, is what the first hybrid shows (213.69 against its 213.0), though the waits were not mainly on the two "att" slots. D's idea, that the wait near 144 us can go, is right, and the kernel before can have it without the change.

**The rule that spoke against the change.** By the row I took 212.2, by the rule of the Trainium skill, "SBUF — State Buffer", section "Who interferes with whom", 213.5. The 217.5 of the measurement lies above both for another reason, the start, so it decides nothing between them. VectorE's steps do behave as the rule says, and I had told only half of it: the section also says that a VectorE step with two inputs in SBUF contends with a GpSimd instruction that reads SBUF, and that one with at most one SBUF input outside the two-port modes does not. The table above agrees row by row (mask 0.68 and 0.83, up to 1.63; x with one operand in PSUM 0.68 and 0.68). The masks stand directly in front of the paired PV groups.
